# A pair less of lead for values and G, two upper shifts for three, and loads behind the shifts, in a neighbourhood attention kernel

## The chip, the cores and the metric

The kernel runs on one core of one Trainium2 chip. Times are device microseconds (us). A run's time is that of the whole execution; the span of a profile goes from its first to its last instruction and is a little shorter. The engines are TensorE (PE, with its weight loads PEld), VectorE (DVE), ScalarE (ACT), GpSimd (POOL) and SyncE (SP, which here only issues transfers). A letter q behind an engine's name means its sequencer.

## The reference

The input is an image `x` of 224 x 224 pixels with 192 channels, in bf16. Each pixel attends to a 7 x 7 neighbourhood with dilation 2, clipped at the border so that it always holds 49 pixels:

```
qkv = x @ wqkv
q, k, v = (qkv[..., :C].copy(), qkv[..., C:2 * C].copy(), qkv[..., 2 * C:].copy())
r0 = jnp.clip(ir - half, 0, H - 1 - (ks - 1) * dil)
c0 = jnp.clip(ic - half, 0, W - 1 - (ks - 1) * dil)
...
logits = jnp.einsum('bnc,bnkc->bnk', qf, kn) * scale
p = _softmax(logits, axis=-1)
o = jnp.einsum('bnk,bnkc->bnc', p, vn) @ wo
```

## The kernel before

**What is computed.** Weights are multiplied together first: A = Wq Wk^T times the scale (tiles `AW`), and Wv Wo (tiles `WP`, `WB`). Then only two products of the image are needed: G = x A, whose inner product with x gives the logits, and V = x Wv Wo, which the probabilities weigh. Since the dilation is 2, rows fall into two classes `rc` by parity, and so do columns (`cc`). The image comes in 14 bands of 16 rows, transposed on the way in (`load_items`, L146, one transposing transfer for each of three channel blocks: `XA[0]`, `XA[1]` and a buffer `X1` that `xb_items`, L159, copies into `XB`). `XB` also carries mask rows, and G carries marks that meet them, so that the mask comes out of the matmul.

**Steps and pairs.** There are 14 steps (a row class and 16 of its rows). A step has 14 slots of 8 column pairs, taken two by two: 7 pairs m = 0 to 6, 98 pairs k in all (k = 7 n + m in step n). The main loop (L679) issues for pair k:

- `stage1` (L479): the logits, PE matmuls of G against XA and XB (L501) into two PSUM tiles `SS`, and their maxima on DVE (L503); `stage1b` (L507): the exponentials on ACT (L512).
- `stage3` and `stage4` of pair k-2 (L534, L550): probabilities times values on PE (L541), read from `VF` and `VD`, then the reciprocals and the scaling on DVE (L547, L564) and the stores (L570 on SP, L593 and short ones on POOL).
- `stage2` of pair k-1 (L515): transposes of the probabilities on PE (L531) and their copy out of PSUM (L532), on DVE but for some pairs of the last step.
- The background work for a later pair: `v_item` (L347), one slot of V: six matmuls (L342, L345) and an evacuation (L335 on ACT or L333 on DVE) into `VF`; `whole` (L441), a group of slots of G; and `halves` (L448), the last 64 channels of a group of G, evacuated to `gx` on ACT and copied into G on POOL (L460). Those PSUM results and those evacuated for the weights share one pool of three buffers (`ps_g`).

**Values and their shift.** The matmul of L541 wants the values of 16 rows that begin 8 rows apart for the two halves of a tile, so there are two copies: `VF`, written by the evacuations, and `VD`, made of it by transfers within SBUF that swap partition halves. `vd_low` (L354) writes VD's lower half from the step's own VF for the step after next; `vd_high` (L358) writes the upper half from the new VF. A step that follows the next one uses the other row class, so VF, VD and G exist twice.

**The lag.** V and G of step n+1 are made in 7 portions `mb` = 0 to 6, of two V slots, one or two `whole` groups and in even portions `halves`. Portion mb goes out in pair k = 7 n + LAG + mb (L685). With LAG 3, portions 4, 5 and 6 of a step's own values fall into its pairs 0, 1 and 2. The upper shift goes out in three pieces: columns 0 to 7 behind V slot 7 (portion 3), 8 to 10 behind slot 10 (portion 5) and 11 to 13 behind slot 13 (portion 6). The background of step 1 is written out by hand: `PLAN` (L610) names for each pair of step 0 its V slots of step 0 (V), those of step 1 (W), `whole` groups of step 0 (G) and 1 (H), each with the engine that evacuates it (a or d), the place of the second `stage4` (N) and an upper shift issued by ACT (T). `AHEAD` says how many W and H are then done. `FIRST` (L619) says in which pair POOL gets its sorts and copies (a to f, k, x, y, g) in steps 0 and 1; from step 2 on a rule at L765 does.

**What sets the order.** Every engine runs its instructions in the program's order (`in_order`, L90). SP's order in a pair is: stores of pair k-2, `vd_low` (L728 to L733), one load (L734), the upper shifts (L750 to L755). A transfer of SP or ACT also waits for the landing of the eighth such transfer before it in the program's order, counted over both. A transfer that waits holds up what its engine is to issue behind it.

The lines that the change and the prediction touch are in the main loop and in the tables ahead of it:

Of the kernel before, what the change touches and what calls it, by code (L numbers as in the profile page):

```python
# [22 lines left out]
NSTEP = 14  # L23
NBAND = 14
# [75 lines left out]
def kernel(  # L100
# [7 lines left out]
    nc = tc.nc  # L108
# [37 lines left out]
    def load_items(b):  # L146

        src = xp[16 * b:16 * b + 16].rearrange("r j c -> (r j) c")
        at = (16 * b) % (2 * RP) * S

        def one(k):
            if k == 1:
                X1[b] = x1_p.tile([128, BND], BF, name=f"x1_{b}", tag="x1")
            dst = X1[b][:] if k == 1 else XA[k // 2][:, at:at + BND]
            nc.sync.dma_start_transpose(out=dst.unsqueeze(1), in_=src[:, 128 * k:128 * k + 128])  # L155

        return [lambda k=k: one(k) for k in ((0, 2, 1) if b in (0, 2, 3) else (1, 0, 2))]
# [189 lines left out]
    def v_item(rc, cb):  # L347
        def emit(dve):
            pv = ps_g.tile([128, 512], F32, name="pv", tag="pg")
            v_mms(pv, lambda k, h: XS[rc][:, k, cb, 64 * h:64 * h + 64])  # L350
            evac(_win(VF[rc], 0, 128, AT[cb] * VP, [[193, 2], [1, C]]), pv[:, 0:2 * C].rearrange("p (t c) -> p t c", c=C), dve)
        return emit
# [5 lines left out]
    def vd_high(rc, c0, c1, eng=nc.sync):  # L358
        eng.dma_start(out=VD[rc][64:128, c0:c1, 0:VP - 1], in_=VF[rc][0:64, c0:c1, 0:VP - 1])
# [147 lines left out]
    def stage1b(J, ab):  # L507
        s_ps, nmx = J.s[ab]
        z = 16 if J.rc == 0 and J.n > 0 else 0
        nr = 16 if J.n == 0 else 14  # L510
        for cc in range(2):
            nc.scalar.activation(out=J.p[:, ab, cc, :, z:z + 8 * nr].rearrange("p q (r k) -> p q r k", k=8), in_=_win(s_ps, 0, 128, cc * 256, [[8, 2], [16, nr], [1, 8]]),  # L512
                                 func=ACTF.Exp, bias=nmx[:, cc:cc + 1], scale=1.0)

    def stage2(J):  # L515
        J.pt = work.tile([128, 8, 128], BF, name="pt_sb", tag="pt_sb")
        if J.k == NP - 1:

            for ab in range(2):
                pt_ps = ps_g.tile([128, 4, 128], BF, name="pt_ps", tag="pg")  # L520
                for i in range(4):
                    for h in range(2):
                        nc.tensor.transpose(pt_ps[64 * h:64 * h + 64, i, :], J.p[:, ab, i // 2, i % 2, 64 * h:64 * h + 64], ident[:])
                nc.vector.tensor_copy(out=J.pt[:, 4 * ab:4 * ab + 4, :], in_=pt_ps[:])
            return
        pt_ps = ps_t.tile([128, 8, 128], BF, name="pt_ps", tag="pt")
        for ab in range(2):
            for cc in range(2):
                for q in range(2):
                    for h in range(2):  # L530
                        nc.tensor.transpose(pt_ps[64 * h:64 * h + 64, 4 * ab + 2 * cc + q, :], J.p[:, ab, cc, q, 64 * h:64 * h + 64], ident[:])  # L531
        (nc.scalar.copy if J.n == NSTEP - 1 and 2 <= J.m < 5 else nc.vector.tensor_copy)(out=J.pt[:], in_=pt_ps[:])  # L532

    def stage3(J, ab):  # L534
        rc, s = J.rc, 2 * J.m + ab
# [61 lines left out]
    for n, (ti, rc) in enumerate(steps):  # L597
        for m in range(7):
            J = Pair()
# [4 lines left out]
    def g_all(n):  # L604
        ti, rc = steps[n]
        its = [g_items(rc, ti, s0, ns) for (s0, ns) in GROUPS]
        return [it for (w0, w1, h) in its for it in (w0, w1)], [h for (w0, w1, h) in its]

    act, dve, pool = nc.scalar.copy, nc.vector.tensor_copy, nc.gpsimd.tensor_copy
    PLAN = (  # L610
        "Vd:0 Vd:1 Vd:2 Ga:2 Gd:3 Va:3 Gd:4 Va:4 Va:5",
        "Gd:5 Vd:6 Xd:0 Xa:1 Vd:7 Va:8 Va:9",
        "Va:10 N- Va:11 Ga:6",
        "Wa:0 Va:12 Wa:1 N-",
        "Hd:0 Wd:2 N- Ga:7 Va:13 Ha:1 Ha:2 Wa:3",
        "Ha:3 Wa:4 Wa:5 N-",
        "Wa:6 N- Wa:7 Ta:0:8 Hd:4",
    )
    FIRST = ("a", "bk", "", "", "cx", "d", "", "", "", "", "", "ge", "y", "f")  # L619

    def first_pool(c):
        if c in SORTS:
# [10 lines left out]
        return [g_marks]  # L633

    SORTS = {"a": (1, 1), "b": (2, 1), "c": (2, 0), "d": (3, 0), "e": (3, 1), "f": (4, 1)}
    LAG = 3
    AHEAD = (8, 5)
    pool_q = []
    end_q = []
    SHORT = {7: 1, NSLOT - 1: 8}  # L640
# [26 lines left out]
    gw0, gh0 = g_all(0)  # L667
# [9 lines left out]
    ld, gw, vs = [], [], []  # L677

    for k in range(NP + 2):  # L679
        J = pairs[k] if k < NP else None  # L680
        n = J.n if J else NSTEP
        w64, w128 = [], []
        if J:
            m = J.m
            nb, mb = divmod(k - LAG, 7)  # L685
            bg = k >= LAG and nb + 1 < NSTEP
            if bg and mb == 0:
                rcb = steps[nb + 1][1]
                gw, gh = g_all(nb + 1)
                vs = [v_item(rcb, cb) for cb in (0, 1, 2, 3, 4, 5, 6, 13, 7, 8, 9, 10, 11, 12)]  # L690
            if bg:
                w64 = gh[mb // 2:mb // 2 + 1] if mb % 2 == 0 else []
            if n == 0 and m < 3:
                w64 = gh0[m + 1:m + 2]
            if bg and n > 0:
                wg, wv = gw[mb + (mb > 1):mb + 1 + (mb > 0)], vs[2 * mb:2 * mb + 2]
                if nb == 0:
                    wg, wv = [it for it in wg if it not in gw[:AHEAD[1]]], [it for it in wv if it not in vs[:AHEAD[0]]]
                w128 = wg + wv
            stage1(J, 0)  # L700
            stage1(J, 1)
            stage1b(J, 0)
            if m == 0 and n + 3 < NBAND:
                ld = load_items(n + 3)
        if k == NP:
            stage2(pairs[k - 1])
        if k >= 2:
            stage3(pairs[k - 2], 0)
            stage3(pairs[k - 2], 1)
            if k >= NP:  # L710
                stage4a(pairs[k - 2], 0)
                stage4a(pairs[k - 2], 1)
            stage4(pairs[k - 2], 0)
            if k == NP - 1:
                stage4a(pairs[k - 2], 1)
        for it in w64:
            it(False)
        if J:
            stage1b(J, 1)
        if 1 <= k < NP:  # L720
            stage2(pairs[k - 1])

        if k >= 2 and n > 0:
            stage4(pairs[k - 2], 1)
        if not J:
            continue

        if m == 1 and 0 < n and n + 1 < NSTEP:  # L728
            vd_low(1 - J.rc, 7, 14)
        if n == 0 and m in (4, 6):  # L730
            vd_low(0, *((0, 4) if m == 4 else (4, 7)), nc.scalar)
        if 0 < n and m in (4, 5) and n + 2 < NSTEP:
            vd_low(J.rc, *((0, 4) if m == 4 else (4, 7)))  # L733
        if ld:  # L734
            ld.pop(0)()
        for w in PLAN[m].split() if n == 0 else ():
            (kind, by), at = w.split(":")[0], [int(c) for c in w.split(":")[1:]]
            if kind in "VWGH":
                {"V": v0, "W": vs, "G": gw0, "H": gw}[kind][at[0]](by == "d")
            elif kind == "N" and k >= 2:  # L740
                stage4(pairs[k - 2], 1)
            elif kind == "X":
                xb_items(2, act if by == "a" else dve)[at[0]]()
            elif kind == "R":
                vd_high(0, at[0], at[1], nc.scalar if by == "a" else nc.sync)
            elif kind == "T":
                vd_high(rcb, at[0], at[1], nc.scalar if by == "a" else nc.sync)
        for it in w128:
            it(False)
            if it is vs[7]:  # L750
                vd_high(rcb, 0, 8)
            if it is vs[10]:
                vd_high(rcb, 8, 11)
            if it is vs[13]:
                vd_high(rcb, 11, 14)  # L755
        if n == 1 and m == 2:
            p_zero(0)
        if n == 0 and m == 1:
            first_vd()
            g_row_on(1, 2, 12)  # L760
            g_col_on()
        if n == 0 and m >= 3:
            marks_on(m % 2, 2 * MM + 3 + (m - 3) // 2)
        add = [it for c in FIRST[k] for it in first_pool(c)] if k < len(FIRST) else []
        if n > 1:  # L765
            if m == LAG and n + 2 < NBAND:
                add = sort_items(n + 2, J.rc, pool)
            if m in (2, 4) and n + 3 < NBAND:
                srt = sort_items(n + 3, J.rc, pool)
                add = srt[:2] if m == 4 else xb_items(n + 3, pool) + srt[2:]  # L770
        pool_q[:0] = add
        if n == 12 and m == 1:
            last = ((0, 9, 0, 1), (9, 7, 9, 0))
            g_col(1, 6, 0, 1, pool)
            g_row(1, 6, 0, 1, pool, last)
            g_row(1, 6, 1, 13, pool, last[1:])
        pool_do(max(4, len(add)))
# [34 lines left out]
```

## Time and profile before

| | us |
|---|---|
| median of 3 runs | 360.17 (360.02 to 360.94) |
| the profiled execution | 361.55 |
| its span | 359.8 |
| PE / DVE / ACT / POOL busy in it | 332.8 / 308.1 / 313.3 / 280.1 |

A line of the profile's waits reads: who waited, for what, us in total, times, longest. A row of the table by stretches reads: from:to in us of the span, its length, then for each engine busy us (instructions), the granted PE clock as a share of full speed, the DMA engines' share, GB/s. A row of the timeline or of the chain reads: start us, us, engine, line, operation, tiles; [idle time ahead of it <- what ended it]. The chain is the work that ended last, followed back from the end; a DMA in it goes from issue to landing.

### The profile page before, as it was taken

How to read it: one execution, taken by the hardware profiler on the slowest of the kernel's cores; microseconds unless marked ns; L12 is line 12 of the kernel's file. 1: busy time of each engine (PE TensorE's matmuls, PEld its weight loads, DVE VectorE, ACT ScalarE, POOL GpSimd, SP SyncE). 2: the span in 40 equal slices, each digit the busy share in tenths (PEclk: the TensorE clock that was granted, in tenths of full speed). 3: DMA queues.
4: the chain of work that ended last, by engine and by line, in shares of the span. 5: the costliest groups of instructions: out<-in, count | busy, mean ns of one | idle time of the engine just before them, and what ended most of it. 6: DMA issues, size and time to landing. Idle time of an engine off the chain costs nothing.

```text
span 359.8 us, 18502 instructions
## 1 busy us (share of the span) xinstructions
PE 332.8 (92%) x7628; PEld 302.1 (84%) x7628; DVE 308.1 (86%) x735; ACT 313.3 (87%) x832; POOL 280.1 (78%) x446
## 2 busy tenths in 40 slices
PE   4599989499999999999999999999999999999982
PEld 2478879389999879999998888889889999999872
DVE  8779889379999888998999889989898898998993
ACT  7669879379999889999999998989898899999993
POOL 8499999994977949949699497795987959483282
PEclk9999999879999999999999999999999999999999
DMA  8999977959989789798896988989979965652534
GB/s 179 214 141 198 152 157 145 191 132 186 191 162 194 157 197 193 158 205 188 153 203 163 191 182 180 180 188 183 195 159 202 176 150 126 136 124 73 121 83 92
DMA packets 136048, 59.35 MB, mean 165 GB/s; under 512 B 88882, under 2 KB 135439, under 8 KB 135964
## 3 DMA queue, kind: packets, MB, share of 16 engines
q1 hardware_dynamic: 129092, 55.33, 76.0%
q0 software_dynamic: 5280, 1.71, 2.8%
q10 hardware_dynamic: 1592, 1.15, 2.1%
q8 instruction: 59, 0.97, 1.2%
q14 instruction: 25, 0.20, 0.2%
HBM read 0.29 MB, written 19.27 MB: 54 GB/s over the span
## 4 chain that ended last, share of the span: by engine, by line
PE 59%; ACT 13%; DMA 13%; DVE 7%; SPq 4%; issue 2%; DVEq 0%; ACTq 0%
PE o_ps L541 12%; PE s L501 12%; DMA vd<-vf 11%; PE pg L425 9%; PE pt_ps L531 8%; PE pv L342 7%; ACT p L512 7%; PE pv L345 6%; PE pgh L425 5%; SPq L155 4%; DVE nmx L503 3%; ACT vf L335 2%; ACT gx L335 2%; ACT g L335 2%; DMA xa<-in_x_dram 1%
## 5 line engine op out<-in xcount | busy, mean ns | idle before, releaser
L512 ACT ACTIVATE p<-s,nmx 128x224 bf16<-128x224 f32 (+1 forms) x392 | 150.9, 452 | 19.7 <-DVE nmx L503 15.2
L503 DVE TENSOR_REDUCE nmx<-s 128x2 f32<-128x392 f32 (+3 forms) x196 | 103.4, 568 | 18.0 <-PE s L501 16.8
L460 POOL COPY g<-gx 64x512 bf16<-64x512 bf16 (+1 forms) x110 | 62.0, 564 | 56.8 <-ACT gx L335 52.8
L564 DVE TENSOR_TENSOR o_sb<-o_ps,rs 128x384 bf16<-128x384 f32 x169 | 94.2, 557 | 6.4 <-DMA out_dram<-o_sb 0.6
L335 ACT CAST vf<-pv 128x384 bf16<-128x384 f32 x197 | 88.9, 524 | 2.8 <-PE pv L345 2.5
L593 POOL DMA_DIRECT2D out_dram<-o_s x150 | 85.1, 573 | 1.0 <-issue 0.8
L541 PE MATMUL o_ps<-vd,pt_sb 128*64 128x193 bf16 x728 | 76.8, 247 | 9.4 <-DMA vd<-vf 6.9
L541 PE MATMUL o_ps<-vf,pt_sb 128*64 128x193 bf16 x840 | 83.2, 247 | 0.0
L501 PE MATMUL s<-xa,g 128*64 128x196 bf16 (+7 forms) x960 | 82.8, 236 | 0.3
L501 PE MATMUL s<-xb,g 128*64 128x196 bf16 (+7 forms) x960 | 82.3, 236 | 0.3 <-ACT g L335 0.3
L541 PEld LDWEIGHTS <-pt_sb 128*64 128x64 bf16 x1568 | 71.6, 109 | 12.2 <-issue 7.3
L501 PEld LDWEIGHTS <-g 128*64 128x64 bf16 x1920 | 78.4, 111 | 1.4 <-issue 0.9
L342 PE MATMUL pv<-wb,xs 128*64 128x384 bf16 x406 | 72.7, 333 | 5.6 <-ACT xs L370 3.5
L532 DVE COPY pt_sb<-pt_ps 128x1024 bf16<-128x1024 bf16 x94 | 64.5, 686 | 14.5 <-PE pt_ps L531 10.9
L345 PE MATMUL pv<-wp,xs 128*64 128x192 bf16 x812 | 73.1, 249 | 0.2 <-issue 0.2
L345 PEld LDWEIGHTS <-xs 128*64 128x64 bf16 x812 | 59.6, 111 | 9.5 <-issue 0.7
L531 PE MATMUL pt_ps<-ident,p 128*64 128x128 bf16 x1552 | 64.3, 220 | 0.0
L531 PEld LDWEIGHTS <-p 128*64 128x64 bf16 x1552 | 57.7, 110 | 5.4 <-issue 0.4
L335 ACT CAST g<-pg 128x512 bf16<-128x512 f32 (+3 forms) x138 | 58.8, 470 | 2.6 <-PE pg L425 2.6
L425 PEld LDWEIGHTS <-aw 128*64 128x64 bf16 x1320 | 55.2, 110 | 4.0 <-issue 1.6
L425 PE MATMUL pg<-xb,aw 128*64 128x512 bf16 (+9 forms) x440 | 55.2, 270 | 0.0
L425 PE MATMUL pg<-xa,aw 128*64 128x512 bf16 (+9 forms) x440 | 52.7, 271 | 1.4 <-DMA xa<-in_x_dram 1.4
(77 smaller groups left out, 351.9 us busy)
## 6 DMA issues: line engine op xcount, KB each, us to landing
out_dram<-o_sb SPq DMA_DIRECT2D x156, 96.0 KB
vd<-vf SPq DMA_DIRECT2D x37, 144.4 KB
vd<-vf SPq DMA_DIRECT2D x12, 385.0 KB
vd<-vf SPq DMA_DIRECT2D x12, 336.9 KB
vd<-vf SPq DMA_DIRECT2D x11, 192.5 KB
out_dram<-o_s POOLq DMA_DIRECT2D x78, 9.0 KB, 3.4
out_dram<-o_sb SPq DMA_DIRECT2D x13, 78.0 KB
out_dram<-xs SPq DMA_DIRECT2D x13, 78.0 KB
```

Source lines behind the costliest of these rows:

```text
L335: nc.scalar.copy(out=out_, in_=in_)
L342: nc.tensor.matmul(pv[64 * h:64 * h + 64, 0:2 * C], lhsT=at(1, h), rhs=WB[:].rearrange("p t c -> p (t c)"), start=True, stop=False, skip_g ...
L345: nc.tensor.matmul(pv[64 * h:64 * h + 64, cc * C:(cc + 1) * C], lhsT=at(2 * cc, h), rhs=WP[(cc, 0)], start=False, stop=True, skip_group_ch ...
L425: nc.tensor.matmul(o, lhsT=l, rhs=r, start=(pas == 0), stop=(pas == 1))
L501: nc.tensor.matmul(o, lhsT=w, rhs=r, start=(pas == 0), stop=(pas == 1))
L503: nc.vector.tensor_reduce(out=nmx[:], in_=_win(s_ps, 0, 128, lo, [[256, 2], [16, 16 if J.n == 0 else 14], [1, 16 - lo]]), axis=AX.XY, op=A ...
L512: nc.scalar.activation(out=J.p[:, ab, cc, :, z:z + 8 * nr].rearrange("p q (r k) -> p q r k", k=8), in_=_win(s_ps, 0, 128, cc * 256, [[8, 2 ...
L531: nc.tensor.transpose(pt_ps[64 * h:64 * h + 64, 4 * ab + 2 * cc + q, :], J.p[:, ab, cc, q, 64 * h:64 * h + 64], ident[:])
L532: (nc.scalar.copy if J.n == NSTEP - 1 and 2 <= J.m < 5 else nc.vector.tensor_copy)(out=J.pt[:], in_=pt_ps[:])
L541: nc.tensor.matmul(o_ps[64 * h:64 * h + 64, cc * 193:cc * 193 + 193], lhsT=J.pt[:, 4 * ab + 2 * cc + q, 64 * h:64 * h + 64], rhs=V[h][:, A ...
L564: nc.vector.tensor_tensor(out=o_sb[:], in0=_win(o_ps, 0, 128, 0, [[194, 2], [1, C]]), in1=rs[:].unsqueeze(2).to_broadcast([128, 2, C]), op ...
L593: pool_q.append(lambda dst=dst, p=p, m=n * nj, cc=cc: nc.gpsimd.dma_start(out=dst.rearrange("j i c -> i j c"), in_=o_sb[p:p + m, cc, :]))
```

## The change

- `LAG` is 2: portion mb of step n+1 goes out a pair earlier. `m == LAG` at L766 becomes `m == 3`, so the sort there stays where it was.
- The upper shift goes out in two pieces: columns 0 to 7 behind slot 7, 8 to 13 behind slot 13.
- The pair's load is issued behind its background and shifts, no longer ahead of them.
- `PLAN`, `FIRST` and `AHEAD` are written anew for the earlier background: 12 W and 6 H instead of 8 and 5 are done in step 0, and the portions' `halves` begin in pair 2.
- In the last step the copy of L532 is on ACT for pairs 1 to 4 instead of 2 to 4.

```diff
-        (nc.scalar.copy if J.n == NSTEP - 1 and 2 <= J.m < 5 else nc.vector.tensor_copy)(out=J.pt[:], in_=pt_ps[:])
+        (nc.scalar.copy if J.n == NSTEP - 1 and 1 <= J.m < 5 else nc.vector.tensor_copy)(out=J.pt[:], in_=pt_ps[:])
...
     PLAN = (
-        "Vd:0 Vd:1 Vd:2 Ga:2 Gd:3 Va:3 Gd:4 Va:4 Va:5",
+        "Vd:0 Vd:1 Va:2 Va:3 Gd:2 Ga:3 Vd:4 Gd:4 Va:5",
         "Gd:5 Vd:6 Xd:0 Xa:1 Vd:7 Va:8 Va:9",
-        "Va:10 N- Va:11 Ga:6",
-        "Wa:0 Va:12 Wa:1 N-",
-        "Hd:0 Wd:2 N- Ga:7 Va:13 Ha:1 Ha:2 Wa:3",
-        "Ha:3 Wa:4 Wa:5 N-",
-        "Wa:6 N- Wa:7 Ta:0:8 Hd:4",
+        "Va:10 Ga:6 Wa:0 N-",
+        "N- Va:11 Wa:1 Wa:2",
+        "Wd:3 Gd:7 Va:12 Vd:13 N- Ha:0 Ha:1 Wa:4",
+        "Wa:5 Ha:2 Wd:6 Wd:7 Ta:0:8 Wd:8 Wa:9 N- Ha:3 Wa:10",
+        "Wa:11 Ha:4 N- Ha:5",
     )
-    FIRST = ("a", "bk", "", "", "cx", "d", "", "", "", "", "", "ge", "y", "f")
+    FIRST = ("a", "bk", "", "x", "", "cd", "", "", "", "g", "f", "e", "y", "")
...
-    LAG = 3
-    AHEAD = (8, 5)
+    LAG = 2
+    AHEAD = (12, 6)
...
             if n == 0 and m < 3:
-                w64 = gh0[m + 1:m + 2]
+                w64 = gh0[m + 1:m + 2] + w64
...
-        if ld:
-            ld.pop(0)()
         for w in PLAN[m].split() if n == 0 else ():
...
             if it is vs[7]:
                 vd_high(rcb, 0, 8)
-            if it is vs[10]:
-                vd_high(rcb, 8, 11)
             if it is vs[13]:
-                vd_high(rcb, 11, 14)
+                vd_high(rcb, 8, 14)
+        if ld:
+            ld.pop(0)()
...
-            if m == LAG and n + 2 < NBAND:
+            if m == 3 and n + 2 < NBAND:
```

## The prediction

> **What bounds the kernel now.** I read the page first, then the waits, then the stretches, then the order of time on SP, ACT and POOL.
>
> ```profile
> PE 332.8 (92%) x7628; PEld 302.1 (84%) x7628; DVE 308.1 (86%) x735; ACT 313.3 (87%) x832; POOL 280.1 (78%) x446
> PE 59%; ACT 13%; DMA 13%; DVE 7%; SPq 4%; issue 2%; DVEq 0%; ACTq 0%
> ```
>
> ```profile
> PE o_ps L541 <- DMA vd<-vf: 6.9, 6, 4.6
> PE o_ps L541 <- DVE nmx L503: 0.8, 1, 0.8
> ```
>
> PE is busy for 92% of the span and holds most of the chain, so time can be won only where PE idles or runs slowly. The waits show one such place that the change touches: PE waits six times, 6.9 us in all, for the shifted values. The seventh wait, 0.8, is put down to DVE, but it stands ahead of a step's first use of the upper shift, and I count it in. The stretches below run from the start of one pair's logits to the next.
>
> ```profile
> 64.30:74.50 10.20, 5.56 (x74) 4.40 (x71) 3.21 (x8) 3.87 (x10) 9.63 (x20) 0.72 1.07 193
> 74.50:77.97 3.47, 3.47 (x68) 3.22 (x66) 2.40 (x6) 2.47 (x7) 3.43 (x4) 0.83 0.48 110
> 94.09:97.45 3.36, 3.36 (x74) 2.96 (x71) 2.73 (x8) 2.94 (x9) 3.30 (x5) 1.00 1.15 152
> 97.45:100.35 2.90, 2.90 (x70) 2.68 (x67) 2.71 (x7) 2.90 (x8) 2.90 (x6) 1.00 0.84 207
> 116.47:120.56 4.09, 3.54 (x73) 2.98 (x70) 2.72 (x8) 2.93 (x9) 4.03 (x6) 1.00 1.21 169
> 77.97:100.35 22.38, 22.36 (x501) 20.25 (x497) 20.47 (x49) 21.12 (x58) 17.16 (x23) 1.00 0.91 180
> ```
>
> Pair 12 (step 1, m = 5) takes 10.20 us; the same pair of step 2 takes 3.36, with the same matmuls. The next takes 3.47 against 2.90. So one event costs 6.84 + 0.57 = **7.4 us**: 10.20 - 5.56 = 4.64 idle, the rest because the granted clock falls (0.72 and 0.83 on average). Pair 26 shows the event in small: 4.09 against 3.36 for 4.09 - 3.54 = 0.55 idle. A step without waits takes 22.38 us (last row), 3.2 a pair, with PE never idle.
>
> ```profile
> 35.81 1.64 SPq L155 DMA_TRANSPOSE x<-in_x_dram  x1
> ...
> 41.79 0.70 SPq L240 DMA_DIRECT2D xb<-xb  x1
> ...
> 58.35 2.54 SPq L570 DMA_DIRECT2D out_dram<-o_sb  x3
> 60.99 0.68 SPq L356 DMA_DIRECT2D vd<-vf  x1
> 61.72 3.48 SPq L155 DMA_TRANSPOSE xa<-in_x_dram  x1
> 65.29 0.63 SPq L359 DMA_DIRECT2D vd<-vf  x1
> ...
> 66.67 1.75 SPq L155 DMA_TRANSPOSE xa<-in_x_dram  x1
> ```
>
> ```profile
> 11.57 5.25 DMA xa<-in_x_dram
> 45.98 3.26 DMA out_dram<-o_sb
> 65.29 4.89 DMA vd<-vf
> 78.16 0.73 PE s L501 x24
> 87.89 0.67 PE s L501 x16
> 113.24 5.01 DMA vd<-vf
> 119.20 0.45 PE pt_ps L531 x16
> 121.43 0.67 PE o_ps L541 x16
> 195.83 4.59 DMA vd<-vf
> ```
>
> From 58.35 on SP works without a gap and issues late: the upper shift of columns 8 to 10 stands behind a load whose issue takes 3.48, goes out at 65.29 and lands 4.89 later, at 70.18; PE, 4.64 idle, has waited since about 65.6.
>
> **The change part by part.** The sum is made against the profiled execution (361.55, span 359.8) and taken over to the median, 360.17, as a difference.
>
> *A, the shift ahead of the load.* The shift of columns 8 to 13 now follows `vd_low` at once, at 61.72. Pieces of three columns took 4.89 and 5.01, one of eight 4.59, so six should take 4.6 to 5.1 and land by 66.9. Meanwhile PE arrives later than 65.6, because with a lag of 2 one more portion of background has been done: 3.2 a pair, less logits 0.67 (the row at 87.89), values 0.67 and transposes 0.45, is 1.4. So PE needs it at about 67 or later, and the wait goes whole: **-7.4** (between -3, if some of it is left, and -7.4). The merged piece also waits for columns 11 to 13, and load and store queue behind it on SP; these columns are now evacuated in the pair that made 10 and 11 before, so I put that at 0 (0 to 1). Loads start one shift issue (0.6) later, hidden while POOL's sorts have slack; uncovered it would be 0.6 a step.
>
> *B, the later waits.* 6.9 - 4.6 = 2.3 and 0.8 make 3.1 idle. Pair 26 lost 0.73 for 0.55, so I scale by 1.33: 4.1. Columns 0 to 7 go out a pair (3.2) earlier, and columns 8 up lose the load ahead of them (2 to 3.5): both exceed the longest wait. **-4.1** (-2 to -4.5).
>
> *C, the first step.* Step 0 gets four V slots and one group of G more to do early. PE has to do them anyway; ACT and DVE, and the three PSUM buffers, must keep up.
>
> ```profile
> 46.76 0.88 ACT L335 CAST vf<-pv 128x384 bf16<-128x384 f32 x2
> 49.31 0.60 ACTq L359 DMA_DIRECT2D vd<-vf  x1
> 49.96 0.79 ACT L512 ACTIVATE p<-s,nmx 128x224 bf16<-128x224 f32 x2 [2.32 <-DVE rs L547]
> 51.27 0.35 PE L342 MATMUL pv<-wb,xs 128*64 128x384 bf16 x2 [1.02 <-ACT gx L335]
> ```
>
> ACT's own upper shift in pair 6 waits for the eighth transfer before it, the store issued at 45.98 that lands at 49.24; ACT stands 2.32, and PE then waits 1.02 for a PSUM buffer. In the changed program that shift is in pair 5 and waits for the mark copy of pair 3, issued at 41.79 in the timeline before; at 3.3 to 5 us it lands at 45 to 47. ACT is with the last evacuations of pair 5 at 46.76 and should come to the shift, which stands ahead of three of them, at about 45. Behind it on ACT stand three evacuations of pair 5 and all of pair 6. Hold and wait stay, moved; the denser pairs make it a little worse: **+0.7** (-1 to +3).
>
> *D, POOL.*
>
> ```profile
> 33.01 1.28 POOL L460 COPY g<-gx 64x512 bf16<-64x512 bf16 x2
> 38.59 2.33 POOL L593 DMA_DIRECT2D out_dram<-o_s  x4
> 41.55 1.81 POOL L171 COPY xs<-xa 128x896 bf16<-128x896 bf16 x2
> 43.30 0.94 POOL L171 COPY xs<-x 128x896 bf16<-128x896 bf16 x1
> 44.18 3.42 POOL L161 COPY xb<-x 64x1792 bf16<-64x1792 bf16 x2
> 69.68 1.80 POOL L171 COPY xs<-xa 128x896 bf16<-128x896 bf16 x2
> 73.85 3.40 POOL L161 COPY xb<-x 64x1792 bf16<-64x1792 bf16 x2
> ```
>
> By 38.59 POOL has done the work that the changed order puts there too. Now the copies of band 3 follow, ahead of the sorts. They need the load of 35.81, which goes out behind the first store (2.54 / 3 = 0.85), at about 36.7, and lands 5.25 or more later: POOL rests from 38.6 to 42, where it sorted before. Then 3.4 of copies, 5.3 of sorts and the issues between put the G copy of group 2 of step 1 at about 58.5, near the time at which pair 10 needs it; C's range covers that. Next, the band 4 sorts can't start before the load issued at 66.67 lands, at about 71.9. From there: 1.8 sort, 0.6 issue, 1.3 G, 2.7 sort, 0.6 issue, 3.4 copies of XB, 1.1 issues, 1.3 G make 12.8: the G copy that pair 17 needs ends at 84.7. Before, pair 17 began at 87.9; less 7.4, plus 0.7 and the 1.4 of work done ahead, PE would be there at 82.6. **+2.1** (0 to +5). After that a step's POOL work (17.2 of 22.38 in the row of step 2) leaves room.
>
> *E, the end.*
>
> ```profile
> 341.57:348.76 7.19, 6.13 (x149) 5.42 (x146) 6.62 (x17) 7.02 (x17) 7.17 (x13) 1.00 0.33 82
> ```
>
> Without background a pair is set by DVE and ACT: three of them leave PE idle for 7.19 - 6.13 = 1.06. There is one more such pair: **+0.4** (0 to 1). The moved copy of L532 keeps DVE and ACT as even there as in the others: 0.
>
> The sum is -7.4 - 4.1 + 0.7 + 2.1 + 0.4 = **-8.3**: span 351.5, execution 353.2, median **351.9**.
>
> [...] The clock fell with a wait of 4.64 and stayed at 1.00 with one of 0.55 (pair 26). [...] Were clock loss not tied to long waits, A would be -4.6 and the sum -5.5.
>
> **The rivals.**
>
> *POOL isn't late* (0.12): the load lands sooner or the G copy is needed later. D and C are 0: 360.17 - 11.1 = 349.1. For it: POOL spans are rough. Against: the queue's length comes row by row.
>
> *The shift is late again* (0.12): SP has no gap in the rows from 58.35; if the new order makes it 4 us later, PE still waits 3 to 4 in pair 12. A shrinks to -4: 355.3. Against: up to the shift SP issues the same transfers.
>
> *POOL's wait becomes the new bound* (0.10): the queue slips 3 more and the wait reaches 5, so the clock falls again: D = 2.1 + 3 + 2.8 = 7.9, so 357.7.
>
> *All of it comes back as other waits* (0.05): within 0.3% of 360.17.
>
> *Slower: values written over a shift that still reads them* (0.11). ACT's evacuation of slots 7 and up overwrites what `vd_low` of columns 7 to 13 reads, and now comes in pair 5 of a step, not 6.
>
> ```profile
> 109.52 0.62 SPq L356 DMA_DIRECT2D vd<-vf  x1
> ```
>
> In step 3 that shift goes out at 109.52 and lands some 4.6 to 5 later, at about 114.3; the evacuation stands behind pair 26's matmuls, which begin at 116.47, so about 119. It decides from a further SP delay of about 4.7 us; from there each us is a us of ACT per step, and ACT has no room (21.12 of 22.38). 6 us later would be 1.3 x 12 steps = 15.6 less 8.3: 367.5. For it: SP lags PE by two pairs in step 1 already. Against: it has one issue less in each step.
>
> **How the numbers follow.** The forecast (350 to 355) has 0.50. The range must leave out no more than 0.2: from 348.5, which takes in the first rival, to 358.0, which takes in the next two; it leaves out about 0.16. A difference under 0.3% (1.1 us) can't be told from none here. Faster by more: 0.50 + 0.12 + 0.12 + 0.10 = 0.84; within: 0.05; slower: 0.11.
>
> **What would show it.** A: pair 12 about 3.4 us long, the upper shift issued right behind `vd_low` near 62, a clock of 1.00 from 60 to 80. B: no row of PE waiting for the shift above 1 us in all. C: a gap on ACT ahead of its shift in pair 5, some 2 us. D: a rest of POOL near 39 to 42, and PE waiting at 80 to 85 for POOL's copies into G or XB. E: five pairs without background at the end. I am wrong if SP's shift of step 1 goes out after 65, if PE's idle time moves into step 0 by more than 3 us, or if ACT waits for SP's transfers in steps 2 to 12.

## The result, and the profile after

| | before | after |
|---|---|---|
| median of 17 runs each, us | 359.47 (356.99 to 361.41) | 356.62 (353.61 to 359.23) |
| profiled execution / span | 361.55 / 359.8 | 357.39 / 355.6 |

The ratio is **0.9929**, 95% interval 0.9904 to 0.9955: about 2.5 us faster, where 8.3 were forecast. The profiled execution of before lies above all 17 timed ones; that of after lies 0.8 above its median. So the profiles differ by 4.2 and the medians by 2.85. The three runs ahead of the prediction lay within 0.92 us of each other; the 17 spread over 4.42. A ratio leaves out runs more than 1.5% above the fastest of the same kernel, so it hangs on that one run, and medians stand beside it where two kernels are close.

The busy line and the chain of the changed kernel, from its page:

```profile
PE 331.6 (93%) x7628; PEld 300.7 (85%) x7628; DVE 307.1 (86%) x736; ACT 311.1 (87%) x831; POOL 279.7 (79%) x446
PE 73%; DMA 7%; ACT 5%; DVE 5%; POOL 3%; SPq 3%; issue 1%; DVEq 0%; ACTq 0%; POOLq 0%
```

DMA fell from 13% of the chain to 7%. The waits say what kind of DMA is left. First a row of the kernel before:

```profile
DVE o_sb L564 <- DMA out_dram<-o_sb: 0.6, 1, 0.6
```

After:

```profile
DVE o_sb L564 <- DMA out_dram<-o_sb: 10.2, 11, 2.4
...
PE o_ps L541 <- DVE o_sb L564: 2.6, 2, 1.6
...
PE o_ps L541 <- DMA vd<-vf: 0.2, 1, 0.2
```

PE's wait for the shift is gone: 6.9 us before, 0.2 now. In its place VectorE waits 10.2 us (0.6 before) for the *stores*: its output (L564) goes into a ring of six buffers `o_sb` (L557), and a buffer is free when its store has landed. While VectorE stands there it doesn't empty the two PSUM buffers of L541, and PE stops (2.6 us in the second row).

Where the time went is read from the stretches pair 0 to 10, 10 to 21, 21 to 91, and 91 to the end. Before:

```profile
17.94:57.91 39.97, 37.69 (x764) 32.56 (x761) 34.39 (x82) 32.90 (x83) 38.59 (x60) 1.00 0.89 158
57.91:100.35 42.44, 37.77 (x786) 33.91 (x783) 32.17 (x77) 33.75 (x92) 36.08 (x58) 0.92 0.91 175
100.35:331.82 231.47, 227.90 (x5495) 211.02 (x5492) 206.34 (x492) 213.27 (x577) 180.77 (x271) 1.00 0.83 170
331.82:359.80 27.98, 20.22 (x473) 17.81 (x468) 20.94 (x56) 21.10 (x51) 12.81 (x22) 0.99 0.42 98
```

After; the last three rows are pairs 12, 13, and 16 with 17:

```profile
18.13:58.92 40.79, 39.44 (x794) 33.91 (x791) 35.97 (x83) 32.99 (x86) 36.58 (x57) 1.00 0.87 156
58.92:99.10 40.18, 36.73 (x776) 31.79 (x773) 32.06 (x80) 33.22 (x92) 35.70 (x58) 1.00 0.94 185
99.10:328.23 229.13, 226.98 (x5503) 211.09 (x5500) 204.85 (x491) 212.05 (x577) 183.16 (x275) 1.00 0.87 172
328.23:355.60 27.37, 18.95 (x446) 16.88 (x440) 20.13 (x53) 20.38 (x49) 12.21 (x21) 0.96 0.43 99
66.29:69.58 3.29, 3.08 (x69) 2.69 (x66) 2.91 (x7) 3.12 (x9) 3.06 (x6) 1.00 1.12 226
69.58:74.81 5.23, 3.58 (x74) 2.80 (x70) 2.15 (x6) 2.86 (x9) 2.14 (x3) 1.00 1.05 170
...
81.42:89.48 8.06, 6.78 (x160) 5.94 (x157) 6.16 (x15) 6.38 (x22) 7.74 (x12) 1.00 0.92 190
```

| stretch | before | after | change | forecast for it |
|---|---|---|---|---|
| up to pair 0 | 17.94 | 18.13 | +0.2 | 0 |
| pairs 0 to 9 | 39.97 | 40.79 | +0.8 | C +0.7, moved portion +1.4 |
| pairs 10 to 20 | 42.44 | 40.18 | -2.3 | A -7.4, D +2.1 |
| pairs 21 to 90 | 231.47 | 229.13 | -2.3 | B -4.1 |
| pair 91 to the end | 27.98 | 27.37 | -0.6 | E +0.4, moved portion -1.4 |
| span | 359.8 | 355.6 | -4.2 | -8.3 |

Pair 12 fell from 10.20 to 3.29 and the clock column stays at 1.00: step A as forecast. But pair 13 takes 5.23 instead of 3.47, and there the shift is not what PE waits for. PE waits for VectorE, and VectorE for a store:

```profile
71.82 0.56 DVE L564 TENSOR_TENSOR o_sb<-o_ps,rs 128x384 bf16<-128x384 f32 x1 [2.35 <-DMA out_dram<-o_sb]
72.43 0.27 PE L541 MATMUL o_ps<-vd,pt_sb 128*64 128x193 bf16 x1 [1.65 <-DVE o_sb L564]
```

SP's order of time behind it:

```profile
61.94 0.66 SPq L356 DMA_DIRECT2D vd<-vf  x1
62.69 0.69 SPq L359 DMA_DIRECT2D vd<-vf  x1
63.44 3.13 SPq L155 DMA_TRANSPOSE xa<-in_x_dram  x1
66.67 0.60 SPq L570 DMA_DIRECT2D out_dram<-o_sb  x1
67.33 1.72 SPq L155 DMA_TRANSPOSE xa<-in_x_dram  x1
69.17 3.81 SPq L570 DMA_DIRECT2D out_dram<-o_sb  x4
```

The shift went out right behind `vd_low`, at 62.69. What it passed, the load, now stands ahead of the stores, and SP, still without a gap, issues these late. The delay has moved from the shift to the stores. It shows over the whole run: from VectorE's end of an `o_sb` (L564) to the start of SP's issue of its store, the median over the stores from 100 to 300 us is 1.89 us before and 2.65 after. The smallest is 0.03 in both, so a store starts to issue as soon as its data is there if SP is free.

### The profile page after: what moved, and what is told of

Its sections match the earlier page's. It is cut to its first block, busy times and chain, and to the rows that moved or that the text cites. A ratio compares the mean times of both kernels' runs of the same rounds, so it can differ in the third digit from the quotient of the medians.

```text
span 355.6 us, 18478 instructions
## 1 busy us (share of the span) xinstructions
PE 331.6 (93%) x7628; PEld 300.7 (85%) x7628; DVE 307.1 (86%) x736; ACT 311.1 (87%) x831; POOL 279.7 (79%) x446
## 2 busy tenths in 40 slices
DMA packets 135839, 59.34 MB, mean 167 GB/s; under 512 B 88674, under 2 KB 135231, under 8 KB 135756
## 4 chain that ended last, share of the span: by engine, by line
PE 73%; DMA 7%; ACT 5%; DVE 5%; POOL 3%; SPq 3%; issue 1%; DVEq 0%; ACTq 0%; POOLq 0%
PE o_ps L541 15%; PE s L501 15%; PE pg L425 12%; PE pt_ps L531 10%; PE pv L342 8%; PE pv L345 7%; PE pgh L425 6%; DMA out_dram<-o_sb 4%; DMA xa<-in_x_dram 3%; SPq L155 3%; ACT p L512 3%; DVE nmx L503 1%; POOL xs L171 1%; DVE o_sb L564 1%; POOL xb L161 1%
## 5 line engine op out<-in xcount | busy, mean ns | idle before, releaser
L503 DVE TENSOR_REDUCE nmx<-s 128x2 f32<-128x392 f32 (+3 forms) x196 | 103.2, 568 | 13.5 <-PE s L501 11.1
L564 DVE TENSOR_TENSOR o_sb<-o_ps,rs 128x384 bf16<-128x384 f32 x169 | 94.2, 557 | 17.0 <-DMA out_dram<-o_sb 10.2
L335 ACT CAST vf<-pv 128x384 bf16<-128x384 f32 x193 | 87.6, 525 | 4.0 <-PE pv L345 2.5
L541 PE MATMUL o_ps<-vf,pt_sb 128*64 128x193 bf16 x840 | 83.3, 247 | 0.1
L541 PE MATMUL o_ps<-vd,pt_sb 128*64 128x193 bf16 x728 | 76.9, 246 | 6.1 <-DVE o_sb L564 2.6
L501 PEld LDWEIGHTS <-g 128*64 128x64 bf16 x1920 | 77.6, 110 | 2.1 <-issue 0.9
L541 PEld LDWEIGHTS <-pt_sb 128*64 128x64 bf16 x1568 | 71.4, 109 | 9.3 <-DVE o_sb L564 3.3
L532 DVE COPY pt_sb<-pt_ps 128x1024 bf16<-128x1024 bf16 x93 | 63.7, 685 | 5.2 <-PE pt_ps L531 1.7
L531 PEld LDWEIGHTS <-p 128*64 128x64 bf16 x1552 | 56.9, 109 | 4.9
L171 POOL COPY xs<-xa 128x896 bf16<-128x896 bf16 x51 | 46.6, 937 | 10.7 <-DMA xa<-in_x_dram 9.2
```

Source lines behind the costliest of these rows:

```text
L335: nc.scalar.copy(out=out_, in_=in_)
L501: nc.tensor.matmul(o, lhsT=w, rhs=r, start=(pas == 0), stop=(pas == 1))
L503: nc.vector.tensor_reduce(out=nmx[:], in_=_win(s_ps, 0, 128, lo, [[256, 2], [16, 16 if J.n == 0 else 14], [1, 16 - lo]]), axis=AX.XY, op=A ...
L532: (nc.scalar.copy if J.n == NSTEP - 1 and 1 <= J.m < 5 else nc.vector.tensor_copy)(out=J.pt[:], in_=pt_ps[:])
L541: nc.tensor.matmul(o_ps[64 * h:64 * h + 64, cc * 193:cc * 193 + 193], lhsT=J.pt[:, 4 * ab + 2 * cc + q, 64 * h:64 * h + 64], rhs=V[h][:, A ...
L564: nc.vector.tensor_tensor(out=o_sb[:], in0=_win(o_ps, 0, 128, 0, [[194, 2], [1, C]]), in1=rs[:].unsqueeze(2).to_broadcast([128, 2, C]), op ...
```

## The experiments

Each ratio is against the kernel before, run on the same chip.

### Is the stall of pair 12 in every execution?

**The kernel before, once more** (no edit).

> The kernel before, unchanged, profiled once more. Theory S (the stall of pair 12 is in every execution, and the changed kernel removes it but meets new waits): pair 12 takes 9.5 to 10.5 us again with the granted clock below 0.9 in it, and the execution 359 to 362. Rival U (the profiled execution of before was an unlucky one, so the forecast summed up a stall that most executions have only in part): pair 12 takes under 8 us or the clock stays at 1.00, and the execution takes under 359.

It took 360.57. Its pairs 10 to 20, pairs 21 to 90, and pair 12:

```profile
56.86:97.66 40.80, 36.61 (x786) 32.90 (x782) 32.12 (x77) 33.49 (x93) 36.16 (x58) 0.96 0.92 184
97.66:330.83 233.17, 227.82 (x5496) 210.63 (x5492) 206.07 (x492) 212.97 (x577) 180.37 (x271) 1.00 0.84 168
...
63.26:72.39 9.13, 4.97 (x74) 3.94 (x71) 3.10 (x8) 3.37 (x9) 8.77 (x20) 0.81 0.96 199
```

The stall is there again, with a clock that falls, 1.1 us smaller and a little below the bound that theory S gave. The executions without a profile say the same by their mean granted clock: in the 94 runs of the kernel before that stand beside the experiments it is 0.991 on average, and below 0.994 in 74 of them; 0.994 is the lowest of the 17 of the changed kernel (0.997 on average). Rival U falls as to its kind: the stall of step A is no chance of one execution, though its full length is.

### The parts of the change by themselves

**Loads ahead of the shifts again, the rest as changed.**

```diff
+        if ld:
+            ld.pop(0)()
         for w in PLAN[m].split() if n == 0 else ():
...
-        if ld:
-            ld.pop(0)()
         if n == 1 and m == 2:
```

> The changed kernel with the loads put back ahead of the shifts of their pair; lag, two transfers and first steps as changed. Theory S: in step 1 the upper shift goes out 3 to 3.5 us later, near 66, lands near 71, and PE, which needs it at 67.6, waits about 3 in pair 12; the other waits for the shift come back in part: 0.997 to 1.004 of the kernel before. Rival L (the order of load and shift means nothing once the lag is 2): 0.990 to 0.996.

0.9959 (0.9926 to 0.9992), median 356.83 against 358.17. Pair 12 in its profile:

```profile
65.44:71.46 6.02, 3.09 (x70) 2.70 (x66) 3.27 (x10) 3.18 (x9) 4.38 (x8) 1.00 1.04 237
```

6.02 - 3.09 = 2.93 idle, as theory S has it (the shift lands late), VectorE waits for stores only 0.2 us in all, and the stores leave 1.64 behind their data at the median, not 2.65 (2.1 to 3.2 in five more profiles with the changed order and lag, further down). So the two orders exchange one wait for the other. The time is Rival L's, not theory S's, and the interval overlaps the changed kernel's: the order is worth nothing that can be told apart.

**Loads behind the shifts, nothing else, in the kernel before** (the same lines moved the other way).

> The kernel before with only the loads moved behind the shifts of their pair (lag 3, three pieces, first steps as before). Theory S: the upper shift of step 1 leaves 3.5 us earlier, near 61.8; PE, with a lag of 3, still comes to it at 65.6 and waits about 1 instead of 4.6, and the clock stays at 1.00: 0.980 to 0.988 by pair 12 alone, and as part of it comes back as waits for store buffers, 0.985 to 0.993. Rival L (the order is worth little; the lag does it): 0.996 to 1.002.

0.9983 (0.9947 to 1.0018), median 358.75 against 359.85. Pairs 12, 13 and 14:

```profile
62.86:67.32 4.46, 3.55 (x74) 2.99 (x70) 2.66 (x7) 2.93 (x9) 4.21 (x13) 1.00 0.93 199
67.32:71.07 3.75, 3.10 (x70) 2.70 (x67) 1.58 (x4) 2.68 (x8) 3.63 (x7) 1.00 1.09 154
71.07:76.64 5.57, 3.82 (x81) 2.81 (x78) 4.15 (x11) 3.15 (x10) 5.41 (x6) 1.00 0.83 206
```

Against the kernel before, once more, pair 12 loses what it was to lose (9.13 to 4.46), and pairs 13 and 14 take 3.75 and 5.57 instead of 2.90 and 3.42: 3.0 of the 4.7 are given back within two pairs, and in the timed runs nothing measurable is left. Theory S was right on the place and wrong on the total, which is Rival L's. From 100 to 300 us the stores leave 1.87 behind their data here, as in the kernel before: with a lag of 3 the order alone doesn't make them later there.

**The upper shift in three pieces again, the rest as changed.**

```diff
-            if it is vs[13]:
-                vd_high(rcb, 8, 14)
+            if it is vs[10]:
+                vd_high(rcb, 8, 11)
+            if it is vs[13]:
+                vd_high(rcb, 11, 14)
```

(and `Td:8:11` behind `Wa:10` in `PLAN`)

> The changed kernel with the upper shift in three pieces again (columns 8 to 10 as soon as they are there, 11 to 13 after), loads behind the shifts. Theory S: in every step one more issue on SP (0.65) ahead of the stores, and the first piece 0 to 3 us earlier than PE needs it anyway: 0.991 to 0.998. Rival P (the merged piece is what PE waits for in the later steps): 0.985 to 0.990.

0.9910 (0.9877 to 0.9943): as the changed kernel. Two transfers or three is nothing that can be measured.

### The ring of store buffers

**A seventh `o_sb`, for the second buffer of the first column group's tile**, in the changed kernel and in the one before.

```diff
-            o_sb = work.tile([128, 2, C], BF, name="o_sb", tag="o_sb", bufs=6)
+            o_sb = work.tile([128, 2, C], BF, name="o_sb", tag="o_sb", bufs=7)
         else:
-            o_sb = work.tile([128, 2, C], BF, name="o_s0", tag="o_s0")
+            o_sb = work.tile([128, 2, C], BF, name="o_s0", tag="o_s0", bufs=1)
```

> The changed kernel with a seventh buffer for the stored outputs (the tile of the first column group, used once per step, gives up its second). Theory S: what was won is partly eaten because VectorE's output (L564) finds no free one of six buffers while SP issues the stores late (10.2 us of such waits in the changed kernel, 0.6 before; PE's idle 1.65 in pair 13 and 2.1 in pairs 49, 55 and 63 end with it). With a seventh the L564 waits fall below 5 us, the idle time in pair 13 below 0.8, and the time to 0.984 to 0.990 of the kernel before. Rival U (there was less to win, and the buffers cost nothing): 0.991 to 0.996, as the changed kernel alone.

> The same seventh buffer in the kernel before. Theory S: there the stores were waited for 0.6 us only, so nothing changes: 0.997 to 1.003. Rival U': the ring costs the kernel before as much as the changed one: 0.990 to 0.996.

1.0248 (1.0200 to 1.0296) and 1.0070 (1.0031 to 1.0110). The buffer that paid was needed: of the first kernel's waits

```profile
DVE o_s L564 <- DMA out_dram<-o_s: 16.3, 5, 7.7
```

(8.9 us in the second). These two runs say nothing on the ring of six.

**The seventh paid for with a staging buffer of G** (`gx`, three to two), **and that alone.**

```diff
-            gx = work.tile([128, 512], BF, name="gx", tag="gx", bufs=3)
+            gx = work.tile([128, 512], BF, name="gx", tag="gx", bufs=2)
```

> The changed kernel with a seventh buffer for the stored outputs, paid for with one of the three staging buffers of G (gx) instead of the first column group's tile, which cost 16.3 us of VectorE's waits in the run before this. Theory S (the wait for store buffers in pairs 13, 49, 55 and 63 eats part of what the shift gave): L564's waits for stores fall from 10.2 to below 5, PE's idle in pair 13 from 1.65 to below 0.8, the time to 0.984 to 0.990 of the kernel before. Rival N (such waits move on to the next thing that SP is late with, or come in some executions only): 0.991 to 0.996.

> The changed kernel with two staging buffers of G instead of three and nothing else, to read the run beside it: POOL waits 33 us for ACT's copies into gx, so the third is hardly used: 0.991 to 0.996 of the kernel before. If ACT then waits for POOL to empty one: 0.997 or more, and the seventh buffer is to be read against this.

0.9934 (0.9896 to 0.9972) with the seventh, 0.9936 (0.9903 to 0.9969) without. In the first, the waits that count read

```profile
PE o_ps L541 <- DMA vd<-vf: 3.0, 3, 2.0
...
DVE o_sb L564 <- DMA out_dram<-o_sb: 1.1, 3, 0.6
```

The wait for stores is gone (10.2 to 1.1), and 3.0 us of waits for the shift are back (0.2 in the changed kernel). That execution took 360.47, 3.5 above the median of its runs, so the rows are read for their kind only. Theory S falls here, since the time stays where Rival N has it: the ring was where the lateness showed, not what made it.

### What is late as a whole: SP's queue and the DMA engines

In the changed kernel, SP's order of time in a quiet stretch:

```profile
192.47 3.58 SPq L570 DMA_DIRECT2D out_dram<-o_sb  x4
196.15 3.30 SPq L155 DMA_TRANSPOSE x<-in_x_dram  x1
199.54 1.19 SPq L570 DMA_DIRECT2D out_dram<-o_sb  x2
200.82 0.63 SPq L356 DMA_DIRECT2D vd<-vf  x1
201.54 0.62 SPq L359 DMA_DIRECT2D vd<-vf  x1
202.21 4.15 SPq L155 DMA_TRANSPOSE xa<-in_x_dram  x1
```

From 192.47 to 206.36 these rows take 13.5 of 13.9 us (a row of several transfers takes in the steps of 0.1 between them). The page's busy line doesn't list it, since issuing is not counted as busy. The DMA share of pairs 21 to 90 is 0.87 in the row further up; whether the engines behind SP are the limit, that share alone doesn't say.

**More bytes, not on SP**: two transfers of 288 KB a step, issued by POOL.

```diff
+        if n > 1 and n + 3 < NBAND and m in (1, 4):
+            nc.gpsimd.dma_start(out=SCR.rearrange("r p c -> p r c"), in_=_win(WB, 0, 128, 0, [[0, 3], [1, 2 * C]]))
```

> The changed kernel, and besides, in steps 2 to 10, two transfers a step of 288 KB each from a constant tile to scratch memory, issued by POOL (0.6 each of POOL's time, SP untouched); the output is the same. Theory Q (the 16 DMA engines are nearly full, share 0.87 to 1.01 in the stretches of steps 1 to 10, so a transfer that is moved ahead makes another late, and the waits only change their names): 9% more bytes lengthen every transfer, and PE's waits for the shift, DVE's for stores and POOL's for loads grow: 1.005 to 1.04 of the kernel before. Theory O (it is SP's order of issue alone that makes things late): 0.991 to 0.997.

1.0300 (1.0242 to 1.0359), nearly all of it in pairs 21 to 90, where PE has no wait for POOL:

```profile
97.17:339.10 241.93, 230.33 (x5503) 209.05 (x5500) 205.17 (x491) 212.17 (x577) 196.31 (x293) 1.00 0.91 183
```

**More transfers on SP, almost no bytes**: two of 4 KB a step.

```diff
+        if n > 1 and n + 3 < NBAND and m in (1, 4):
+            nc.sync.dma_start(out=SCR, in_=_win(WB, 0, 128, 0, [[1, 16]]))
```

> The changed kernel with two more transfers a step on SP in steps 2 to 10, of 4 KB each, behind the load of pairs 1 and 4: they take SP 0.6 each, as the two of 288 KB took POOL, and next to nothing of the DMA engines. Theory Q (the bytes made that run 12 us slower, through full engines): 0.991 to 0.998. Theory O (what fills SP's time makes everything late): 1.005 or more.

1.0178 (1.0125 to 1.0232), where theory Q had 0.991 to 0.998:

```profile
98.30:337.62 239.32, 230.57 (x5504) 209.42 (x5501) 204.56 (x491) 211.62 (x577) 183.16 (x275) 1.00 0.83 166
```

18 issues of 0.59 are 10.6 us of SP's time, and the stretch is 239.32 - 229.13 = 10.2 longer. By the ratios it is 1.0178 - 0.9929, some 9 us. Bytes are not needed for the loss; time on SP is enough.

**Two of the three loads of each band left out from band 7 on**, in the changed kernel and the one before.

```diff
-                ld = load_items(n + 3)
+                ld = load_items(n + 3)[:3 if n + 3 < 7 else 1]
```

> The changed kernel with two of the three loads of each band left out from band 7 on (those into XA, so the computation goes on with older rows of x and only its time means anything). Theory Q: from step 4 on the DMA share falls below 0.75 and the lost time of pairs 28 to 90, some 3.5 us, falls below 1: 0.980 to 0.986. Theory R (what is left is lost to VectorE and ACT, whatever the DMA engines do): 0.989 to 0.996.

> The kernel before with two of the three loads of each band left out from band 7 on (its computation goes on with older rows of x, only the time means anything). Theory Q: as in the changed kernel, what is lost after pair 28 (5 to 7 us in the two profiles of it) falls below 1.5, so 0.981 to 0.987, and the distance to the changed kernel with the same loads left out (0.989) closes. Theory O: the shift still stands behind the stores and the third load: 0.990 to 0.998.

0.9891 (0.9831 to 0.9950) and 0.9823 (0.9764 to 0.9883). Pairs 21 to 90 of the changed one:

```profile
97.05:323.92 226.87, 226.30 (x5503) 211.39 (x5500) 206.09 (x491) 212.99 (x578) 182.95 (x275) 1.00 0.69 146
```

Idle time there falls from 2.2 to 0.6 (length less PE's busy time), as theory Q has it; but there was less to win than the 3.5 it counted on, and the ratio of the changed kernel lies in Theory R's range. In the kernel before the stretch falls to 227.34. Relieved, the two are within 0.5 us of each other in these 70 pairs: neither lag nor order is worth more there.

**Two of the 13 large stores of a step issued by POOL** (same bytes, less on SP).

```diff
-                    put(nc.gpsimd if nj < 8 and s % 2 == 1 else nc.sync)
+                    put(nc.gpsimd if (nj < 8 and s % 2 == 1) or (nj >= 8 and J.n > 1 and s in (3, 9)) else nc.sync)
```

> The changed kernel with two of the 13 large stores of each step (slots 3 and 9, from step 2 on) issued by POOL instead of SP. Theory P (SP's queue is the third full engine: whatever is put on it or taken off it shows in the time, as the two small transfers a step did, 9 us for 18 of them): about as much comes off, as far as there is something to win: lost time of pairs 21 to 90 from 4 to below 2, 0.985 to 0.990 of the kernel before. Theory Q (the DMA engines' bytes): 0.991 to 0.996. If POOL, held at a store until VectorE has written it, comes late with G: 0.997 or more.

0.9919 (0.9881 to 0.9958), median 355.49 against 359.94. VectorE's waits for stores in these pairs fall from 7.0 to 1.6, but the stretch is 228.71 in its profile, with 1.52 of what is lost in one stop that nothing released, and the ratio is Theory Q's and can't be told from the changed kernel's. Inconclusive for theory P.

### Larger packets for the shift

**Whole rows**: 386 elements of a column instead of 385, so that a partition's columns are one run.

```diff
-        eng.dma_start(out=VD[rc][0:64, c0:c1, 0:VP - 1], in_=VF[rc][64:128, c0:c1, 0:VP - 1])
+        eng.dma_start(out=VD[rc][0:64, c0:c1, :], in_=VF[rc][64:128, c0:c1, :])
```

(and so in `vd_high`), in the changed kernel and in the one before.

> The changed kernel with the shifts taking whole rows (386 elements of each column instead of 385; the last is zero on both sides), so that a partition's columns are one run of memory and not one packet of 770 B each. Theory Q: some 1,800 packets a step fewer, shifts land 1 to 2 us sooner, and everything behind them: 0.982 to 0.990. Rival: the bytes count and not the packets, nothing moves: 0.991 to 0.996.

> The kernel before with shifts that take whole rows (386 elements a column, one run a partition) and nothing else: lag 3, three pieces, loads first. Theory Q (the DMA engines are nearly full, and whatever is late is late through them): PE's waits for the shift after pair 20 fall from 2.3 to 5 us to below 1, that of pair 12 from 4.2 to about 3, as the load's issue still stands ahead of it: 0.986 to 0.993. Theory O (SP's order): the waits stay: 0.996 to 1.003.

0.9866 (0.9812 to 0.9919), median 353.13 against 359.80, and 0.9852 (0.9803 to 0.9900), median 354.29 against 360.09. Packets fall from 135,839 to 117,407, and a shift's issue from 0.63 to 0.55. The kernel before with whole rows, pairs 21 to 90 and pair 12:

```profile
99.08:325.69 226.61, 226.18 (x5497) 211.79 (x5492) 206.33 (x492) 213.35 (x577) 180.83 (x272) 1.00 0.85 173
...
63.67:73.72 10.05, 5.56 (x74) 4.40 (x70) 3.21 (x8) 3.87 (x10) 9.59 (x22) 0.67 0.98 193
```

All of B's waits vanish (the stretch falls by 4.9, to 0.4 idle) with lag 3, three pieces and loads first; the stall of pair 12 stays, since there the load's issue stands ahead of the shift.

**Another order of POOL's work** in steps 0 and 1 (in this order sort c writes over rows of `XS[0]` that two V tiles of step 0 have still to read, so these tiles hold other rows; only its time is read).

```diff
-    FIRST = ("a", "bk", "", "x", "", "cd", "", "", "", "g", "f", "e", "y", "")
+    FIRST = ("a", "bk", "", "c", "", "xd", "", "", "", "g", "e", "f", "y", "")
```

> The changed kernel with POOL's work of the first steps in another order (sort c ahead of the copies of band 3, sort e ahead of f), so that POOL neither rests near 39 nor is late for pairs 16 and 17. Theory S' (those two waits are a cost of the new order by themselves, 1.3 idle, 1.7 in the lengths of the pairs): 0.986 to 0.991, POOL waiting under 1 near 39 to 42, PE not waiting for POOL near 84. Rival: the time is taken by the transfers that come next: 0.991 to 0.996.

0.9962 (0.9905 to 1.0019), median 358.88 against 359.80. The waits of pairs 16 and 17 for POOL are gone; instead

```profile
PE pv L342 <- POOL xs L171: 2.6, 1, 2.6
```

PE waits in pair 4 for sort c. One wait was sold for another, here by the edit itself.

**Whole rows, and only sorts e and f changed about.**

```diff
-    FIRST = ("a", "bk", "", "x", "", "cd", "", "", "", "g", "f", "e", "y", "")
+    FIRST = ("a", "bk", "", "x", "", "cd", "", "", "", "g", "e", "f", "y", "")
```

> The changed kernel with whole rows in the shifts, and POOL's sorts e and f of the first steps changed about, so that the sort whose load lands last (f, band 4) comes after the other and POOL does not rest ahead of it. POOL then finishes the copies for pairs 16 and 17 1.5 to 2.7 us sooner and PE's waits of 1.04 and 0.31 there go: 0.982 to 0.986 of the kernel before, against 0.987 without. If another wait takes their place: 0.986 to 0.990.

**0.9806** (0.9760 to 0.9852), median 352.33 against 360.09: faster than both kernels, though not clear of whole rows alone (0.9812 to 0.9919). PE's wait in pair 16, 1.04 with whole rows alone, is 0.44.

**That, and two stores on POOL.**

> The same two stores on POOL, in the changed kernel with whole rows in the shifts and POOL's sorts e and f changed about (0.981 of the kernel before). Theory P: with whole rows next to nothing is waited for after pair 21 but instruction issue (2.7 lost), so little more can be won: 0.978 to 0.983. If POOL comes late: 0.984 or more.

0.9854 (0.9808 to 0.9901), median 353.46 against 359.94: nothing more to win. The number lies where a late POOL was to put it, but PE waits for POOL only 0.3 twice.

Put side by side, from the traces: how long SP is at work in the 200 us from 100 to 300 (the summed time of its instructions that begin there), how far the start of a store's issue lies behind the end of its data on VectorE (median), and the length of pairs 21 to 90, of which PE needs at least 226 (its busy time in the rows above). The 228.58, 228.71 and 228.37 hold 2.3, 1.5 and 1.7 of stops that nothing released.

| kernel | SP at work | stores behind their data | pairs 21 to 90 |
|---|---|---|---|
| before, after | 177.8, 178.9 | 1.89, 2.65 | 231.47, 229.13 |
| after, 288 KB more on POOL; 4 KB more on SP | 185.6, 185.0 | 3.93, 3.95 | 241.93, 239.32 |
| whole rows: before, after | 167.5, 163.9 | 0.92, 0.58 | 226.61, 228.58 |
| after, two stores on POOL | 161.8 | 0.92 | 228.71 |
| that, with whole rows and sorts e and f changed about | 150.9 | 0.31 | 228.37 |
| loads left out: before, after | 137.5, 138.2 | 0.03, 0.03 | 227.34, 226.87 |

In the changed kernel SP is at work for 89% of the time, and its stores start 2.65 behind their data at the median. It rests only 7.2 of the 200 us (pauses over 0.15; the other 13 are short steps from one instruction to the next), and 1.4 and 1.1 with the additions, at 93%, which cost 10 us and more. At 82 to 84%, with whole rows, the stores start 0.58 and 0.92 behind their data. With 288 KB more on POOL SP too spends more of the time issuing, 185.6 for 178.9, though it issues nothing more. **Shown**: SP's time alone is enough to lengthen the kernel, by about as much as is put on it (10.6 put on, 10.2 longer); what is taken off it goes with fewer waits in both kernels (whole rows: SP 10.3 and 15.0 less at work, the stores 0.97 and 2.07 closer behind their data); and changes of order gave nothing that the timed runs show. What decides is not SP's waiting for the landing of earlier transfers: such pauses are at most 1.1 of the 200 us in any of the 20 profiles. **Open**: why one issue takes longer than another of the same kind (in the changed kernel a store from 0.54 to 2.13, a load into XA from 1.67 to 4.68), and so how much of SP's time is made by the DMA engines.

## Why the prediction was wrong, point by point

- **What bounds the kernel**: PE, and its waits for the shift, were read rightly. The rows of SP from 58.35, "without a gap", were in the text, but taken as a matter of step 1 and of what stands ahead of one transfer.
- **A (-7.4)**: right as to the wait and its clock. Pair 12 gave 6.9, the upper shift left at 62.69 behind `vd_low`, the clock stayed at 1.00. The step that failed is the term for what comes behind the shift: "load and store queue behind it on SP ... I put that at 0 (0 to 1)". In its place the stores cost +1.8 in pair 13 and from 100 to 300 us they leave later (2.65 behind their data, 1.89 before). The other pairs from 10 to 20, 16 and 17 apart, are 1.1 longer together; PE waits only 0.2 in them, so the cause of that part is open.
- **B (-4.1)**: failed by the same step. The waits for the shift did go (0.2 left, no row above 1 us), but nothing was put down for what is late next. The stores were: VectorE's waits for them in pairs 21 to 90 rose from 0.6 to 7.0, and the stretch gave 2.3. With a seventh buffer in the ring, or with the loads first, it was the shift again.
- **C (+0.7) and E (+0.4)**: with the portion moved, +2.1 and -1.0 were forecast, +0.8 and -0.6 came; together +0.2 for +1.1. ACT's gap at its shift in pair 5 came at 1.48 instead of some 2 us: ACT stands from 44.69 to 46.17, with the issue of 0.60 at 45.46 in it.
- **D (+2.1)**: right. POOL rests 2.86 from 38.8 on, PE waits 0.95 for the copies of XB in pair 16 and 0.31 for G in pair 17, and the two pairs take 8.06 instead of 6.32: +1.7. The sum puts no loss of clock on D's wait of 2.1, and no run shows that term: a wait of 2.93 over two steps of the clock left it at 1.00, idle time of 2.04 within one was followed by half clock (last section), and what came was 0.95 and 0.31 with the clock at 1.00.
- **From the profile to the median**: the difference was carried over as it stood. The profile gave -4.2 and the medians -2.85, since the profiled execution of before was slower than any of the 17. That part of the miss is bad luck with the execution that was profiled.
- **The rivals**: POOL was late; the shift was not late again; POOL's wait didn't grow to a new bound; the overwriting of VF that `vd_low` reads cost nothing (ACT has no wait for a transfer of SP in steps 2 to 12). "All of it comes back as other waits", at 0.05, was nearest to what happened: about half came back, and with only the order changed in the kernel before all of it.

## What to carry to other kernels

Ask of a late transfer whether *it* is late or its queue. If the queue that issues it has no gaps (sum the time of its instructions; the busy line leaves it out, and a row of several transfers holds the steps between them), an earlier place for one transfer is a later place for the next (here the stores, from 1.89 to 2.65 behind their data), and the gain is to be sized by the next buffer that isn't free; here only work taken off the queue was won (larger packets: the median falls by 5.8 us in the kernel before, and by 3.5 in the changed one, there between two chips). How far a store's issue starts behind its data showed the lateness at once (2.65, and 0.58 with whole rows). And a kernel whose executions spread by 2 us needs the wait in more than one profile before its whole length goes into a sum.

## What the runs showed of the hardware

**When the granted clock fell.** In all 20 traces 3.41 us or a whole multiple of it (6.83, 23.89, 283.31) lie from one change of the granted clock to the next. Each trace was cut into steps of 3.41, back from its last change, and PE's idle time taken within each step. Between 17 and 348 us, all eight steps at full clock with 2.04 us or more of it were followed by half clock, and none with 1.90 or less was. The shortest, in the kernel with a seventh `o_sb` and two `gx`:

```profile
288.85:292.26 3.41, 1.37 (x46) 1.25 (x44) 1.37 (x4) 1.24 (x4) 2.46 (x5) 1.00 0.64 171
292.26:295.67 3.41, 3.41 (x62) 3.41 (x59) 1.59 (x4) 2.52 (x8) 2.71 (x6) 0.50 0.79 170
```

The wait of 2.93 in pair 12 with the loads first is longer, but falls into two steps, 1.72 and 1.21 idle, and the clock stays:

```profile
65.03:68.44 3.41, 1.69 (x38) 1.51 (x35) 2.83 (x8) 3.16 (x9) 3.23 (x8) 1.00 0.96 192
68.44:71.85 3.41, 2.20 (x48) 1.98 (x49) 1.24 (x3) 0.81 (x2) 1.54 (x3) 1.00 0.98 238
71.85:75.26 3.41, 3.41 (x82) 3.01 (x79) 3.05 (x8) 3.04 (x9) 2.98 (x5) 1.00 0.58 124
```

So in these runs the length of a wait alone doesn't tell whether the clock falls: 2.93 over two steps left it at 1.00, 2.04 within one was followed by 0.50. Why it changes at these steps is not shown.

**The time of an issue beside its bytes.** In the kernel with 4 KB more, one issue on SP takes 0.59 for 4 KB, 0.56 for a store of 96 KB and 0.62 for a shift of 144 to 385 KB (medians). 18 of 288 KB on POOL, another queue, cost 241.93 - 229.13 = 12.8 us, 0.71 each.

**Stops that nothing released.** In six of the 14 profiles with lag 2 PE stops 0.5 to 1.7 us, once or twice, somewhere from 152 to 161, which the trace puts down to issue alone (1.52 in the one with two stores on POOL); in the six with lag 3 there is none at that place. What it is, is open.
